# Fused set attention and gated FFN on one core: first batch's stages sorted by the time they can begin, last 24 tiles in six parts of four, idle matmuls in TensorE's wait

One core of one Trainium2 chip. The metric is the device time of one execution in microseconds (us); lower is better. The "span" of a trace is the core's own time from its first to its last instruction, some 1.8 us less.

## The reference

Two attentions in a row (each a batch's tokens against 32 inducing points), then a gated FFN on every token:

```python
def _attn_ref(x, inducing):                  # x: 4 x 12416 x 128, inducing: 32 x 128
    I = np.broadcast_to(inducing[None], (B, m, C))
    def mab(q, kv):
        s = scale * (q @ kv.transpose(0, 2, 1))
        s = s - s.max(-1, keepdims=True)
        a = np.exp(s)
        a /= a.sum(-1, keepdims=True) + 1e-09
        return a @ kv
    h = mab(I, x)                            # "first attention"
    return mab(x, h)                         # "second attention"

def _moe_ref(x, w_gate, w_val, w_out):       # 49664 x 128, d_ff 1536
    gate = np.maximum(x @ w_gate, 0.0)
    val = x @ w_val
    return gate * val @ w_out
```

## The kernel before

The body (the FFN of a batch, and beside it the attention of the next) is one long software pipeline. The change is in what comes ahead of it, the **head**: all of batch 0 has to be loaded (97 tiles of 128 tokens), cast to fp16, transposed, scored against the inducing points, exponentiated and summed, before the first score of the second attention (L178) can begin. A part of the load passes through these stages:

```python
sizes = [8] * 10 + [4] * 3 + [2] * 2           # tiles in each load; the single tile 96 is put in as part 3
...
def turn(j):                                    # transposes (L268, PE) and their copy out of PSUM (L269, DVE)
    for t in range(t0, t1):
        nc.tensor.transpose(ps[:, t - t0, :], x16[:, t, :], eye16)
    nc.vector.tensor_copy(out=xTs(xT, t0, t1 - t0), in_=ps[:, 0 : t1 - t0, :])

for j in range(n_parts + 3):
    if j < n_parts:                             # casts of part j: half on POOL (L280), half on ACT (L281)
        ...
        nc.gpsimd.tensor_copy(out=dst[:, 0:h, :], in_=x32[:, 0:h, :])
        nc.scalar.copy(out=dst[:, h:, :], in_=x32[:, h:, :])
    ...                                         # scores (L290, PE) and exp (L292, ACT) of part j-2
    ...                                         # sums of part j-3 on PE: z1a (L301), z (L311), hT (L314)
    if j < n_parts - 1:
        turn(j)
    ...
idle(idle_ps, 3, ...)                           # three matmuls whose result nobody reads (L262)
hT = finish_h(hT_ps, z1)                        # reciprocal L145, product L147 (DVE)
s2 = s2_pe(hT, xT, (0, 1, 0, 1))                # L178: the second attention, and with it the body, begins
```

So the order on each engine is fixed: casts of part j, scores of part j-2, sums of part j-3, transposes of part j.

The softmax here doesn't subtract the row's maximum and nothing guards it: scores larger than these inputs give would overflow.

## Time and profile before

| Kernel before | |
|---|---|
| three runs ahead of the prediction | 700.35, 700.41, 700.72 us |
| profiled execution | 700.71 us, span 698.9 us, recorded clock of TensorE 0.997 |
| last x tile cast, by POOL | 20.78 us |
| first score of the second attention (L178) | 26.05 us |

In the lines below, the first number is the start in us from the start of the span, the second the busy time of that row, then engine, line, operation, out<-in, shape and count; in brackets stands how long the engine was idle before and what ended the wait.

```profile
5.47 1.03 PE L268 MATMUL xT_ps<-eye,x 128*128 128x128 f16 x8 [0.89 <-POOL x L280]
...
9.06 0.27 PE L301 MATMUL z1a_ps<-p,ones 128*128 128x256 f16 x1
```

Eight transposes take 1.03 us at 5.47, and 0.62 at 14.65 in the prediction's lines. So the kernel begins at half clock too; a z1a matmul of 256 columns takes 0.37 at half clock and 0.27 at full, which makes these rows a clock that can be read off the timeline. In this execution the clock is up by 9.06. (The packed trace's record of clock changes begins with the rise itself, at 8.79; the views count the time before that as full clock.)

### The profile page before, as it was taken

The numbers are of one execution on the slowest core, as the hardware profiler recorded it, in microseconds if no ns is written. First come the engines' busy times: TensorE is split into PE (matmuls) and PEld (weight loads), VectorE is DVE, ScalarE is ACT, GpSimd is POOL, SyncE is SP. The second block draws the span as 40 slices with busy tenths as digits, with TensorE's granted clock in tenths as the row PEclk, the third lists the DMA queues.
The fourth block names the chain that finished last, engine by engine and source line by source line (L and its number), as shares of the span: only waits on it lengthen the run. The fifth ranks groups of instructions, "written<-read, shape, count | busy, mean of one in ns | idle before, by whom it ended". The sixth has DMA issues, their size and how long they took to land.

```text
span 698.9 us, 13946 instructions
## 1 busy us (share of the span) xinstructions
PE 631.5 (90%) x4552; PEld 181.1 (26%) x4552; DVE 676.8 (97%) x617; ACT 672.7 (96%) x1380; POOL 372.5 (53%) x680
## 2 busy tenths in 40 slices
PE   5999998999999999999999999998999898888897
PEld 4522222222222222222222222222222222222224
DVE  4699999999999999999999999999999999999997
ACT  5699999999999999999999999999999999999996
POOL 3628648655186474665247474773424543534443
PEclk9999999999999999999999999999999999999999
DMA  9647876432565957513287785732223231231233
GB/s 349 218 122 175 175 166 169 119 78 67 136 174 156 198 146 170 129 61 77 61 173 189 197 185 139 142 99 70 68 70 85 58 92 56 80 84 53 76 56 91
DMA packets 142633, 87.57 MB, mean 125 GB/s; under 512 B 117184, under 2 KB 125920, under 8 KB 140256
## 3 DMA queue, kind: packets, MB, share of 16 engines
q1 hardware_dynamic: 142368, 86.60, 48.8%
q8 instruction: 35, 0.57, 0.3%
q14 instruction: 38, 0.31, 0.2%
q10 hardware_dynamic: 192, 0.08, 0.0%
HBM read 27.80 MB, written 25.43 MB: 76 GB/s over the span
## 4 chain that ended last, share of the span: by engine, by line
ACT 40%; PE 25%; issue 19%; DVE 13%; DMA 2%; SPq 0%; ACTq 0%; POOL 0%; DVEq 0%
ACT g L982 30%; DVE gv L994 13%; PE o_ps L674 11%; PE v_ps L885 8%; ACT oT L680 6%; PE g_ps L885 3%; DMA gv<-in_x_dram 2%; ACT p2q L194 2%; ACT p1T L533 2%; PE o_ps L741 1%; ACT hgv L169 1%; PE h_ps L599 0%; PE xT_ps L268 0%; PE idle_ps L262 0%; ACT p L189 0%
## 5 line engine op out<-in xcount | busy, mean ns | idle before, releaser
L994 DVE TENSOR_TENSOR gv<-g,v_ps 128x1024 f16<-128x1024 f16 (+1 forms) x578 | 657.2, 1209 | 3.3 <-ACT g L982 1.0
L982 ACT ACTIVATE g<-g_ps 128x512 f16<-128x512 f32 (+1 forms) x1168 | 603.2, 618 | 6.7 <-PE g_ps L885 2.5
L674 PE MATMUL o_ps<-gv,wo 128*128 128x512 f16 x1128 | 352.4, 384 | 45.9 <-ACT oT L680 45.8
L691 POOL TENSOR_SCALAR osb<-o,z2i 128x128 f32<-128x128 f16 x380 | 165.8, 453 | 228.7 <-DMA o<-oT 217.1
L885 PE MATMUL g_ps<-p,hgv 32*128 32x512 f16 x1152 | 282.4, 379 | 0.8 <-ACT g L982 0.5
L885 PE MATMUL v_ps<-p,hgv 32*128 32x512 f16 x1152 | 223.6, 384 | 5.5 <-DVE gv L994 4.3
L885 PEld LDWEIGHTS <-hgv 32*128 32x128 f16 x2400 | 66.8, 91 | 267.2 <-issue 262.9
L674 PEld LDWEIGHTS <-wo 128*128 128x128 f16 x1176 | 80.8, 97 | 212.4 <-issue 198.6
L430 POOL TENSOR_TENSOR z2i<-zt,minus 128x16 f32<-128x16 f32 (+3 forms) x31 | 73.3, 2367 | 0.5
L680 ACT CAST oT<-o_ps 128x512 f16<-128x512 f32 (+1 forms) x98 | 59.1, 603 | 0.1
L423 POOL TENSOR_TENSOR zt<-zt 128x32 f32<-128x32 f32 (+5 forms) x124 | 35.1, 283 | 9.7
L501 POOL CAST x<-x 128x2048 f16<-128x2048 f32 x18 | 34.1, 1892 | 11.4 <-DMA x<-in_x_dram 10.8
L423 POOL TENSOR_TENSOR zt<-p2T 128x256 f32<-128x256 f16 (+3 forms) x31 | 17.5, 563 | 30.7 <-DMA p2T<-p 15.4
L269 DVE COPY xT<-xT_ps 128x1024 f16<-128x1024 f16 (+2 forms) x15 | 8.7, 585 | 9.6 <-PE xT_ps L268 8.6
L577 POOL TENSOR_TENSOR zq<-p1g 128x256 f32<-128x256 f16 x18 | 12.1, 671 | 8.5 <-DMA p1g<-p1T 8.5
L280 POOL CAST x<-gv 128x512 f16<-128x512 f32 (+2 forms) x14 | 7.6, 548 | 11.8 <-DMA gv<-in_x_dram 11.7
L281 ACT CAST x<-gv 128x512 f16<-128x512 f32 (+2 forms) x14 | 7.6, 545 | 6.3 <-DMA gv<-in_x_dram 6.3
L268 PE MATMUL xT_ps<-eye,x 128*128 128x128 f16 x97 | 10.0, 254 | 3.8 <-POOL x L280 3.1
L194 ACT ACTIVATE p2q<-s_ps 128x512 f16<-128x512 f32 x22 | 13.4, 610 | 0.0
L579 POOL TENSOR_TENSOR zq<-zq 128x256 f32<-128x256 f32 x15 | 10.9, 726 | 1.2
L533 ACT ACTIVATE p1T<-s1T_ps 128x512 f16<-128x512 f32 x18 | 11.0, 611 | 0.0
L178 PE MATMUL s_ps<-xT,hT 128*32 128x512 f16 x108 | 10.8, 389 | 0.2
(94 smaller groups left out, 159.2 us busy)
## 6 DMA issues: line engine op xcount, KB each, us to landing
out_dram<-osb SPq DMA_DIRECT2D x95, 256.0 KB, 2.2
x<-in_x_dram SPq DMA_DIRECT2D x18, 1024.0 KB, 5.8
p<-p2q SPq DMA_DIRECT2D x88, 64.0 KB, 2.0
gv<-in_x_dram SPq DMA_DIRECT2D x10, 512.0 KB, 7.1
o<-oT SPq DMA_TRANSPOSE x98, 2.4
gv<-in_x_dram SPq DMA_DIRECT2D x3, 256.0 KB, 10.6
x<-in_moe_w_out_dram SPq DMA_DIRECT2D x1, 768.0 KB, 8.1
x<-in_moe_w_gate_dram SPq DMA_DIRECT2D x1, 512.0 KB, 5.3
```

Of the source, the lines that this page charges most:

```text
L194: nc.scalar.activation(out=p2q, in_=ps, func=AF.Exp, scale=sm_scale)
L423: nc.gpsimd.tensor_tensor(out=dst, in0=v[:, :, :, 0:m], in1=v[:, :, :, m : 2 * m], op=ALU.add)
L430: nc.gpsimd.tensor_tensor(out=z2i, in0=v[:, :, :, 0], in1=minus1[:, 0 : n * g].rearrange("p (n g) -> p n g", n=n), op=ALU.pow,)
L501: nc.gpsimd.tensor_copy(out=s["x16"][:, t0:t1, :], in_=s["x32", q])
L533: nc.scalar.activation(out=p1T, in_=ps, func=AF.Exp, scale=sm_scale)
L577: add(out=z, in0=s["p1g"][q][:, 0:half, :], in1=s["p1g"][q][:, half:, :], op=ALU.add)
L674: nc.tensor.matmul(c["ps"][:, 0:w], wo[:, i, :], gv(i), start=(i == 0), stop=(i == NFF - 1))
L680: nc.scalar.copy(out=oT[:, 0:w], in_=c["ps"][:, 0:w])
L691: nc.gpsimd.tensor_scalar(out=osb[:, t, :], in0=o16[:, t, :], scalar1=zz, scalar2=zz, op0=ALU.mult, op1=ALU.mult,)
L885: nc.tensor.matmul(ps[:, cols], hgv[:, s * P : (s + 1) * P], p2, start=True, stop=True)
L982: nc.scalar.activation(out=g16[:, k * w : (k + 1) * w], in_=ps[:, 0:w], func=AF.Relu)
L994: nc.vector.tensor_tensor(out=dst[:, ks, :], in0=g16[:, ks, :], in1=v[:, ks, 0:w], op=ALU.mult)
```

## The change

Its intent: let each stage stand in the queues where its input should be there by an estimated time, rather than at a fixed distance in parts; make the last parts small and equal; and keep TensorE busy in the wait where x arrives late, so that its clock isn't halved.

```diff
-    sizes = [8] * 10 + [4] * 3 + [2] * 2
+    sizes = [8] * 9 + [4] * 6
...
-    n_big = n_parts - 2
+    n_big = sum(t1 - t0 in (8, 1) for t0, t1 in parts)
...
-    for j in range(n_parts + 3):
-        ...                                    # the loop above
+    def cast(j): ...
+    def score(j): ...                          # p1 has 4 buffers, was 3
+    def sums(j): ...
+    def reduce(j): ...
+    late = [j for j in range(n_parts) if parts[j][0] >= 64 and parts[j][1] < NT][0]
+    for j, (t0, t1) in enumerate(parts):
+        n = t1 - t0
+        landed += n
+        at = 0.16 * landed + (1.4 if j >= late else 0)
+        stages.append((at - (0.6 if j == n_parts - 1 else 0), 0, j, cast))
+        at += 0.1 + 0.065 * n
+        if j == late:
+            idles = lambda j: idle(idle_ps, 3, xT[0][:, 0:4, :].rearrange("p t c -> p (t c)"))
+            stages.append((at, 1, j, idles))
+        stages.append((at, 2, j, turn))
+        if j == n_parts - 1:
+            stages.append((at + 0.3, 3, j, reduce))
+        at += 0.05 * n + 0.5 + 0.068 * n + (0.6 if n > 4 else 0.15)
+        stages.append((at, 3, j, score))
+        at += 0.025 * n + 0.6 + 0.026 * n + (0.6 if n > 4 else 0.3)
+        stages.append((at, 4, j, sums))
+    for _, _, j, f in sorted(stages, key=lambda e: e[0:3]):
+        f(j)
...
-                hq = st([P, P], FP32, "hq", 2)
+                hq = st([P, P], FP32, "hq", 1)
```

`at` is a hand-written model of when data are there: 0.16 us a tile, and a pause of 1.4 us ahead of the part that begins at tile 64.

More of the change, by code (lines that the diff above doesn't have):

```diff
@@ L269, in turn @@
         nc.vector.tensor_copy(out=xTs(xT, t0, t1 - t0), in_=ps[:, 0 : t1 - t0, :])
-    for j in range(n_parts + 3):
-        if j < n_parts:
-            t0, t1 = parts[j]
-            x32 = x32s[j]
-            dst = x16[:, t0:t1, :]
-            if t1 == NT:
-                nc.vector.tensor_copy(out=dst, in_=x32)
-            elif j < n_parts - 1:
-                h = (t1 - t0) // 2
-                nc.gpsimd.tensor_copy(out=dst[:, 0:h, :], in_=x32[:, 0:h, :])
-                nc.scalar.copy(out=dst[:, h:, :], in_=x32[:, h:, :])
-            if j == n_parts - 2:
-                t0, t1 = parts[j + 1]
-                nc.gpsimd.tensor_copy(out=x16[:, t0:t1, :], in_=x32s[j + 1])
-        for i in {n_parts: (j - 2, j - 1), n_parts + 1: ()}.get(j, (j - 2,) if 1 < j < n_parts else ()):
-            t0, t1 = parts[i]
-            ps = bank("g", "s1_ps", [P, 8, M])
-            for t in range(t0, t1):
-                nc.tensor.matmul(ps[:, t - t0, :], xTs(xT, t, 1), indT, start=True, stop=True)
-            p1 = p1s[i] = st([P, 8, M], FP16, "p1", 3)
-            nc.scalar.activation(
-                out=p1[:, 0 : t1 - t0, :], in_=ps[:, 0 : t1 - t0, :], func=AF.Exp, scale=sm_scale
-            )
-        if j > 2:
-            t0, t1 = parts[j - 3]
-            p1, n = p1s[j - 3], t1 - t0
-            if j == n_parts + 2:
-                nc.tensor.matmul(z1, ones32[0:1, :], z1s[0:1, :], start=False, stop=False)
-            if j - 3 < n_big:
-                nc.tensor.matmul(
-                    z1a[:, 0 : n * M],
-                    ones16,
-                    p1[:, 0:n, :].rearrange("p t m -> p (t m)"),
-                    start=j == 3,
-                    stop=j - 3 == n_big - 1,
-                )
-            end = j == n_parts + 2
-            for t in range(n if j - 3 >= n_big else 0):
-                first, last = j - 3 == n_big and t == 0, end and t == n - 1
-                nc.tensor.matmul(z1, ones16, p1[:, t, :], start=first, stop=last)
-            for t in range(n):
-                first, last = j == 3 and t == 0, end and t == n - 1
-                nc.tensor.matmul(hT_ps, x16[:, t0 + t, :], p1[:, t, :], start=first, stop=last)
-        if j < n_parts - 1:
-            turn(j)
-        if j == n_parts - 2:
-            turn(j + 1)
-        if j == n_parts:
-            z1s = st([P, M], FP32, "z1s", 1)
-            nc.vector.tensor_reduce(
-                out=z1s, in_=z1a.rearrange("p (t m) -> p m t", m=M), axis=AX.X, op=ALU.add
-            )
@@ new lines, in cast, with score @@
+    def cast(j):
+        t0, t1 = parts[j]
+        x32, dst, n = x32s[j], x16[:, t0:t1, :], t1 - t0
+        if n == 1:
+            nc.vector.tensor_copy(out=dst, in_=x32)
+            return
+        h = n // 2 if n != 4 or j == n_parts - 1 else 2
+        nc.gpsimd.tensor_copy(out=dst[:, 0:h, :], in_=x32[:, 0:h, :])
+        if h < n:
+            nc.scalar.copy(out=dst[:, h:, :], in_=x32[:, h:, :])
+    def score(j):
+        t0, t1 = parts[j]
+        n = t1 - t0
+        ps = bank("g", "s1_ps", [P, 8, M])
+        for t in range(n):
+            nc.tensor.matmul(ps[:, t, :], xTs(xT, t0 + t, 1), indT, start=True, stop=True)
+        p1s[j] = st([P, 8, M], FP16, "p1", 4)
+        nc.scalar.activation(out=p1s[j][:, 0:n, :], in_=ps[:, 0:n, :], func=AF.Exp, scale=sm_scale)
@@ new lines, in sums @@
+    def sums(j):
+        t0, t1 = parts[j]
+        p1, n, end = p1s[j], t1 - t0, j == n_parts - 1
+        if j == n_parts - 2:
+            nc.tensor.matmul(z1, ones32[0:1, :], z1s[0:1, :], start=False, stop=False)
+        if j < n_big:
+            nc.tensor.matmul(
+                z1a[:, 0 : n * M],
+                ones16,
+                p1[:, 0:n, :].rearrange("p t m -> p (t m)"),
+                start=j == 0,
+                stop=j == n_big - 1,
+            )
+        for t in range(n if j >= n_big else 0):
+            first, last = j == n_big and t == 0, end and t == n - 1
+            nc.tensor.matmul(z1, ones16, p1[:, t, :], start=first, stop=last)
+        for t in range(n):
+            first, last = j == 0 and t == 0, end and t == n - 1
+            nc.tensor.matmul(hT_ps, x16[:, t0 + t, :], p1[:, t, :], start=first, stop=last)
@@ new lines, in reduce @@
+    def reduce(j):
+        nc.vector.tensor_reduce(
+            out=z1s, in_=z1a.rearrange("p (t m) -> p m t", m=M), axis=AX.X, op=ALU.add
+        )
+    z1s = st([P, M], FP32, "z1s", 1)
+    stages = []
+    landed = 0
+    late = [j for j in range(n_parts) if parts[j][0] >= 64 and parts[j][1] < NT][0]
+    for j, (t0, t1) in enumerate(parts):
+        n = t1 - t0
+        landed += n
[12 more added lines that the diff above has]
+        stages.append((at, 4, j, sums))
```

## The prediction

> **What bounds the kernel now.** I read the page's chain of work that ended last, then the busy time by window, then the timeline of the first 28 us. The chain shows that the body belongs to other code:
>
> ```profile
> ACT g L982 30%; DVE gv L994 13%; PE o_ps L674 11%; PE v_ps L885 8%; ACT oT L680 6%; PE g_ps L885 3%; DMA gv<-in_x_dram 2%; ACT p2q L194 2%; ACT p1T L533 2%; PE o_ps L741 1%; ACT hgv L169 1%; PE h_ps L599 0%; PE xT_ps L268 0%; PE idle_ps L262 0%; ACT p L189 0%
> ```
>
> The lines of the change (L268 transposes, and the first batch's scores and sums) have less than 1% each. The busy time by window for the stretch after the first batch says why:
>
> ```profile
> 100.00:650.00 550.00, 503.16 (x3429) 132.83 (x3426) 549.12 (x484) 544.94 (x1117) 297.40 (x534) 1.00 0.47 116
> ```
>
> Columns: window, length, then PE, weight load, DVE, ACT, POOL busy, clock, DMA share, GB/s. DVE is busy 549.12 of 550.00 us. That work is not touched, so the change can only start this body earlier. Its worth is what it takes from the head. Next the timeline of the head, each row with start, duration, line, and in brackets the idle time before:
>
> ```profile
> 14.65 0.62 PE L268 MATMUL xT_ps<-eye,x 128*128 128x128 f16 x8 [0.16 <-POOL x L280]
> ...
> 17.48 0.62 PE L268 MATMUL xT_ps<-eye,x 128*128 128x128 f16 x8 [1.70 <-POOL x L280]
> ...
> 20.07 0.59 PE L268 MATMUL xT_ps<-eye,x 128*128 128x128 f16 x4
> ...
> 20.78 0.40 POOL L284 CAST x<-gv 128x256 f16<-128x256 f32 x1
> ...
> 22.73 0.69 PE L268 MATMUL xT_ps<-eye,x 128*128 128x128 f16 x4
> ...
> 24.24 0.42 DVE L321 TENSOR_REDUCE z1s<-z1a_ps 128x32 f32<-128x256 f32 x1 [0.49 <-PE z1a_ps L301]
> ...
> 25.31 0.36 DVE L145 RECIPROCAL rz<-z_ps 128x32 f32<-128x32 f32 x1 [0.64 <-PE hT_ps L314]
> ...
> 26.05 0.40 PE L178 MATMUL s_ps<-xT,hT 128*32 128x512 f16 x4
> ```
>
> The last x tile is cast at 20.78 to 21.18, but its transpose starts only at 22.73 or a little later, and the first score of the second attention (L178), which starts all the rest, at 26.05. From data to start are 26.05 - 20.78 = 5.27 us. Between 18.77 and 22.74 the chain by time runs without a break through PE. Two things make PE late: it idled 1.70 us for data at 15.8 to 17.5, and it then ran slowly:
>
> ```profile
> 15.63:19.04 3.41, 1.54 (x36) 1.33 (x33) 1.07 (x2) 1.88 (x5) 1.50 (x3) 1.00 1.06 381
> 19.04:22.45 3.41, 3.41 (x66) 3.22 (x64) 1.54 (x3) 2.04 (x7) 2.55 (x7) 0.50 1.03 359
> 12.22:15.63 3.41, 3.23 (x80) 3.01 (x76) 2.12 (x4) 2.17 (x5) 1.23 (x2) 1.00 1.02 402
> ```
>
> I cut these windows at the edges where the clock changed. PE was busy 45% (1.54 of 3.41) in the first, and had half the clock in the whole of the next.
>
> **What the Trainium skill says.** "TensorE: Matmul & The Clock Gate", section "What's actually happening": the clock is halved or restored after free-running windows of 3413 ns, by how busy PE was. The trace agrees: half clock lasted from about 19.04 to 22.45. The same page, "Wait — 56ns, not 53.3ns?": start to start never falls below about 25 ns however small the matmul. The trace agrees: at half and at full clock eight 32-column scores put the next instruction 0.20 to 0.21 us on. So the half clock hurts the transposes and the 256-column sums, not the 32-column ones. "PSUM — Partial Sum Buffer", "Engine vs sequencer instructions": ACT, DVE and POOL queues are strict FIFO and matmuls keep program order. The trace is in keeping with it, so the issue order is the schedule. "DMA: Bandwidth & Descriptors", "Specifications", puts the ceiling at 435 GB/s; the trace has 413 GB/s at 8.8 to 12.2 us, so the loads are near it and cannot be hurried.
>
> **The change, part by part.**
>
> (1) Sizes: nine parts of 8 tiles, the single tile, six of 4, against ten of 8, three of 4, two of 2. Still 16 loads and the same bytes; the last data should land near 20.75 as now. The first of the new small parts covers tiles 72 to 75, half of what landed at 18.06; I place it at 17.42 (halfway from 16.78). Estimated landings of the six: 17.42, 18.06, 18.73, 19.41, 20.09, 20.75. Cost of more parts: the last 24 tiles now have six copies of 0.42 us on DVE (2.52) against 0.69 + 3 x 0.42 + 2 x 0.29 = 2.53: nothing. Sums of the six parts no longer use a 128 or 256-column matmul but 24 matmuls of 32 columns, 24 x 0.025 = 0.6 us of PE, spread out.
>
> (2) Idle matmuls: three of 512 columns before the transposes of tiles 64 to 71. By the same form later (25.17, three in 0.81 us) they fill 0.8 of the 1.70 us wait, and the score and sums before them fill 0.6 more, so PE's next window is busy about 2.9 of 3.41 us (an estimate), as the windows that kept the clock were (79 to 95%). What that is worth: 20 transposes at 107 instead of 56 ns (0.43 against about 0.22 for four), 1.0 us, and three 256-column sums at 0.21 instead of 0.11, 0.3 us: 1.3 us of PE's queue.
>
> (3) Order: by it, the scores and sums stand where their input should be there, rather than at fixed distances of two and three parts; transposes of new tiles stand earlier. To price it I walked the queues in the printed instruction order of the changed kernel, with durations of the trace: 4-tile cast 0.40, ACT free again some 0.08 earlier; transposes of four 0.23 on PE, DVE copy starting 0.44 after their start, 0.42 long, next copy 0.05 later; score of four 0.10 on PE, exp 0.30 after its start, 0.28 long (eight tiles 0.38); sums of four 0.20, of eight 0.32 on PE. A through F are the six small parts, "9" the part of tiles 64 to 71.
>
> - 17.45 transposes 9, copy to 18.79. A's copy queues behind it on DVE to 19.26, B's to 19.73.
> - Score A 19.31, exp A to 19.89. The cast of D landed at 19.41 but stands behind exp A on ACT: done 20.21.
> - Score 9 waits for a PSUM bank that copy B frees: 19.78; score B 19.98. exp 9 to 20.51, exp B to 20.70; on ACT the casts of E and F follow, done 21.02 and 21.34. exp C is behind them: 21.54.
> - Transposes D 20.25; sums A; score C 20.68; transposes E 21.06; sums B; score D 21.49.
> - Transposes F need the bank that exp C frees: 21.59; copy F to 22.45, reduction of the big sums to 22.92.
> - PE: sums 9, sums C, score E, sums D from 21.82 to 22.64; score F 22.64, exp F to 23.22.
> - Sums E with the joining fp32 matmul (0.33 by L299 to L311) 22.97 to 23.50; sums F 23.50. The last sum of z is ready some 0.31 later, the reciprocal starts at 23.81.
> - From reciprocal to L178 it is 26.05 - 25.31 = 0.74 us now, and unchanged: 24.55.
>
> The head ends 26.05 - 24.55 = **1.5 us earlier**. The lower limit of such a tail, with nothing in the way after the last cast at 21.18: transposes and copy 0.9, score and exp 0.63, sums 0.5, then 0.74, gives 23.95, a gain of 2.1 us. The walk loses 0.6 of it to ACT's and PE's order.
>
> (4) Buffers: a fourth p1 buffer costs no time; hq falls from two to one. An hq is written once per pair of chunks, 28 slots of some 1.15 us apart, about 32 us, and read by one POOL addition right after: no wait.
>
> Sum: 700.41 - 1.5 = **698.9 us**.
>
> **The rivals.**
>
> *The weights become the bound.* After x come the weight loads, whose end the change does not move. The first halves are cast by 22.72, before 24.55; the last of the gate and value weights by 26.34 (25.30 plus 1.04), needed by the second L159 group at 28.91 now, 27.4 then. 1.1 us are left, so I expect no wait, though the whole gain of the lower limit would leave only 0.5. If it did bind, the gain would stop at about 1: 699.4.
>
> *The clock falls later.* The windows run freely. The tail has gaps for data and banks on PE; if a window still counts too little, the half clock only moves to the stretch with the last sums, L178, L159 and the idle matmuls, which cost about 0.8 us more there (ten 512-column passes at 0.21 extra would be 2.1, of which the idle ones lie partly in waits). Gain 0.7: 699.7. Against it: no window with PE over 79% busy lost the clock.
>
> *The order is worse than the old one in places.* ACT is strictly in order, and the last cast (F) stands before exp C, which waits for nothing; if data land later than I placed them, everything on ACT shifts. A slip of 0.5 us in the landings gives 699.4.
>
> *The order is better than my walk.* If copies and banks come sooner, up to 698.3.
>
> *The body swallows it.* If in the first slots something fixed in time (the output weights' cast at 27.55 to 29.02, the first loads of the next batch) set the pace, nothing would be gained: 700.4. Against it: the output weights are needed only from slot 10, past 40 us, and the DVE rows from 30.41 on are unbroken.
>
> **Range and chances.** 698.9 with 0.8 either way: the lower end is the limit of the tail (2.1) plus a little run noise (the three runs span 0.37), the upper end has the clock or order rivals. 2% would be 14 us, more than half the head: faster and slower by over 2% have 1% each, and slower only if the buffer reduction in (4) stalled the body, for which I see no path.
>
> **What would show each step.** Right: half-clock slices gone between 19 and 22.5 us; L178's place near 24.5 us; the last x cast still at about 20.8 to 21.3; idle matmuls end before the transposes of tiles 64 to 71; DVE in the body as busy as before and the body as long. Step (2) wrong: clock below 0.9 in any window from 17 to 28 us. Step (3) wrong: clock full, but L178 later than 25.2. The weights rival: POOL's L325 as releaser of PE at the second L159. Wrong altogether: L178 earlier by over a microsecond and the span not.

## The result, and the profile after

Ratios here and below are the mean time of one kernel's fast runs over that of the other's of the same rounds, so not quite the ratio of the medians beside them.

| | runs (us) | median |
|---|---|---|
| before | 700.35, 700.41, 700.72, 699.03 | 700.38 |
| after | 699.82, 699.53, 700.17, 700.41 | 700.00 |

Ratio 0.9998 (95%: 0.9981 to 1.0015): the same time. The prediction had 698.9, range 698.1 to 699.7; the measured 700.0 lies outside.

The body was left alone, as predicted. Busy time by window of the kernel after (columns as in the prediction's window lines):

```profile
100.00:650.00 550.00, 503.74 (x3431) 132.84 (x3431) 549.12 (x484) 545.03 (x1117) 297.61 (x539) 1.00 0.46 116
```

DVE is busy 549.12 of 550 us, the same to the last digit. The half clock of the tail is gone. By single microseconds, before:

```profile
20.00:21.00 1.00, 1.00 (x25) 0.94 (x22) 0.62 (x2) 0.61 (x3) 0.86 (x3) 0.50 0.86 332
21.00:22.00 1.00, 1.00 (x23) 0.94 (x22) 0.36 (x2) 0.72 (x3) 0.74 (x2) 0.50 1.01 395
```

and after:

```profile
20.00:21.00 1.00, 0.93 (x20) 0.79 (x21) 0.74 (x3) 0.57 (x3) 0.73 (x2) 1.00 1.01 397
21.00:22.00 1.00, 0.93 (x24) 0.82 (x23) 0.46 (x2) 1.00 (x6) 0.68 (x2) 1.00 1.01 400
```

The eighth column is the clock: 0.50 against 1.00. Yet L178 has come from 26.05 only to 25.10, not to 24.55. The timeline of the head after shows where it was held up:

```profile
8.70 1.14 PE L268 MATMUL xT_ps<-eye,x 128*128 128x128 f16 x9 [0.70 <-DVE x L275]
...
9.91 0.37 PE L297 MATMUL z1a_ps<-p,ones 128*128 128x256 f16 x1
...
11.72 0.37 PE L297 MATMUL z1a_ps<-p,ones 128*128 128x256 f16 x1
...
13.52 0.28 PE L297 MATMUL z1a_ps<-p,ones 128*128 128x256 f16 x1
...
15.25 1.10 POOL L278 CAST x<-gv 128x512 f16<-128x512 f32 x2 [0.66 <-DMA gv<-in_x_dram]
...
17.61 0.38 ACT L289 ACTIVATE p<-s_ps 128x256 f16<-128x256 f32 x1 [0.57 <-PE s_ps L287]
...
17.68 0.81 PE L262 MATMUL z1a_ps<-xT,eye 128*128 128x512 f16 x3
17.89 1.53 ACT L280 CAST x<-gv 128x512 f16<-128x512 f32 x4
...
19.24 0.40 POOL L278 CAST x<-gv 128x256 f16<-128x256 f32 x1 [1.56 <-DMA gv<-in_x_dram]
...
20.59 0.40 POOL L278 CAST x<-gv 128x256 f16<-128x256 f32 x1 [0.26 <-DMA gv<-in_x_dram]
...
24.35 0.36 DVE L145 RECIPROCAL rz<-z_ps 128x32 f32<-128x32 f32 x1 [0.89 <-PE z_ps L306]
...
25.10 0.40 PE L178 MATMUL s_ps<-xT,hT 128*32 128x512 f16 x4
```

Four things differ from what I had walked through.

- **The half clock at the start lasts until about 13.5 us**, not 9. The z1a rows show it (0.37, 0.37, 0.28), and the clock record has the rise at 13.58. In the walk everything ran at full clock.
- At 8.0 PE stands idle for 0.70 us: the transpose of the single tile is now ahead of that of tiles 16 to 23, and waits for a cast on DVE.
- **The late part is another one.** Tiles 64 to 71 land at about 15.2 (POOL casts them at 15.25), without a pause. The pause comes before tiles 84 to 87 (POOL idle 1.56 us until 19.24). The order assumes it ahead of tile 64.
- ACT casts its half of tiles 64 to 71 only at 17.89, 2.6 us after the data, since in its fixed order the cast stands behind exps of earlier parts, which wait for PE (17.61); PE fills the time with the idle matmuls (17.68), for data that have long been there.

What was right: POOL cast its half of the last x part from 20.59 (landing predicted at 20.75), and from reciprocal to L178 it is 25.10 - 24.35 = 0.75 us (predicted 0.74). ACT's half of that part was done only at 22.05, where the walk had 21.34.

**The distance from L178 to the end is fixed.** Span less start of L178 is 698.9 - 26.05 = 672.85 before and 698.0 - 25.10 = 672.90 after, and 672.85 to 672.96 in all 16 usable traces. So L178's place tells the time of an execution, and nothing of the gain was lost in the body.

### The profile page after: what moved, and what is told of

It reads as the page before. It is cut to its first block, busy times and chain, and to the rows that moved or that the text cites. A ratio compares the mean times of both kernels' runs of the same rounds, so it can differ in the third digit from the quotient of the medians.

```text
span 698.0 us, 13986 instructions
## 1 busy us (share of the span) xinstructions
PE 632.2 (91%) x4571; PEld 181.2 (26%) x4571; DVE 676.6 (97%) x617; ACT 672.8 (96%) x1381; POOL 370.9 (53%) x680
## 4 chain that ended last, share of the span: by engine, by line
ACT 39%; PE 21%; issue 18%; DVE 12%; DMA 7%; POOL 2%; SPq 0%; ACTq 0%; POOLq 0%; DVEq 0%
ACT g L998 29%; DVE gv L1010 12%; PE o_ps L690 10%; PE v_ps L901 7%; ACT oT L696 5%; PE g_ps L901 3%; DMA x<-in_x_dram 2%; DMA gv<-in_x_dram 2%; ACT p2q L194 2%; DMA x<-in_moe_w_out_dram 1%; ACT p1T L549 1%; PE o_ps L757 1%; DMA o<-oT 1%; ACT hgv L169 1%; DMA out_dram<-osb 1%
## 5 line engine op out<-in xcount | busy, mean ns | idle before, releaser
L269 DVE COPY xT<-xT_ps 128x1024 f16<-128x1024 f16 (+1 forms) x15 | 8.6, 584 | 9.0 <-PE xT_ps L268 8.4
L278 POOL CAST x<-gv 128x512 f16<-128x512 f32 (+1 forms) x15 | 7.9, 528 | 11.7 <-DMA gv<-in_x_dram 11.6
L289 ACT ACTIVATE p<-s_ps 128x256 f16<-128x256 f32 (+2 forms) x16 | 5.2, 333 | 6.1 <-PE s_ps L287 5.9
L280 ACT CAST x<-gv 128x512 f16<-128x512 f32 (+1 forms) x15 | 7.4, 532 | 3.7 <-DMA gv<-in_x_dram 3.7
```

## The experiments

There were 15 runs in four groups, on two chips: of eleven new kernels, and of the kernels before and after again. The first three groups have their own runs of the kernel before; the fourth uses the nine of the third and one more. All kernels gave the right result. In most executions the time is 1.7 to 2.0 us more than the span, in some up to 3.0; why isn't shown, so the larger comparisons below use spans. "Clock up by" is the first z1a or score row of the timeline that has the full-clock duration.

The theories at this point, in words: the *pause* theory (the order's pause stands ahead of the wrong part, and a right guess gives the predicted 1.5 us); the *two kinds* theory (the kernel before has two kinds of execution, and I had profiled the slow one); the *beginning* theory (the order is held up by its start, the single tile or the clock). The expectations are quoted as they were written ahead of each group; where they letter theories, the letters are those of that group.

### First group: repeat, and parts of the change (before: nine runs, median 699.41)

**The kernel after again (r_after).**

> The changed kernel once more, unaltered, for more runs and a second trace. Theory A (the head is 0.95 us shorter in every execution, the four first runs were only too few against a spread of 1.7 us): L178 near 25.1 us again, and 0.6 to 1.2 us faster than the kernel before in five rounds. Rival B (the gain is in some executions only, because the late load falls elsewhere in others): L178 anywhere between 24.5 and 26, the times as spread as before and no difference over 0.4 us.

Measured: 699.71, 699.65, 700.01, 701.27, and 2523.82 for the profiled execution, which was spoilt and isn't used. Ratio 1.0010 (0.9996 to 1.0024). In this group the kernel before was at 699.4, not 700.4, and the kernel after stayed where it had been.

**Idle matmuls alone, in the old kernel (e_idle).**

```diff
+            if parts[j][0] == 64:
+                idle(idle_ps, 3, xT[0][:, 0:4, :].rearrange("p t c -> p (t c)"))
         if j < n_parts - 1:
             turn(j)
```

> The kernel before with the three idle matmuls alone, ahead of the transposes of tiles 64 to 71, in the old order and sizes. Theory A (of the 0.95 us most was the half clock): no half clock from 19 to 22.5 us, L178 near 25.0 to 25.2, so as much as the whole change. Rival B (the clock costs little since the tail waits for data anyway): L178 at 25.6 to 26.0, though the clock is full.

Measured: 699.15 to 699.36 in five of five (ratio 0.9997, 0.9985 to 1.0010), L178 at 24.66, no half clock in the tail. Timeline of this kernel:

```profile
9.09 0.37 PE L301 MATMUL z1a_ps<-p,ones 128*128 128x256 f16 x1
...
15.85 0.81 PE L262 MATMUL z1a_ps<-xT,eye 128*128 128x512 f16 x3
16.49 0.61 PE L268 MATMUL xT_ps<-eye,x 128*128 128x128 f16 x8
...
24.66 0.40 PE L178 MATMUL s_ps<-xT,hT 128*32 128x512 f16 x4
```

So L178 is 26.05 - 24.66 = 1.4 us earlier than in the trace of before, and earlier than either theory had it. Not all of that need be the matmuls': a second halved trace (r_before, below) has 25.39. Yet the time is hardly better than that of the nine runs of before. Their recorded clocks say why. Two of the nine have 0.997 and 0.998, and 700.14 and 700.39 us; the other seven have 0.999 or 1.0, and a mean of 699.38. **The kernel before has two kinds of execution**, with and without a window of half clock in its tail, and both its time and the profile that I had read were of the halved kind.

**The change without its idle matmuls (e_noidle).**

```diff
-            stages.append((at, 1, j, idles))
```

> The changed kernel without the three idle matmuls. In its trace they ran at 17.68 to 18.49, where PE would have waited for ACT's cast of tiles 64 to 71 at 18.3 in any case. Theory A (the new order alone keeps PE busy enough in every window): clock full, L178 within 0.15 us of 25.1. Rival B (the idle matmuls hold the clock): a stretch of 3.4 us at half clock somewhere from 19 to 26 us, and L178 at 25.6 to 26.2.

Measured: 699.79, 699.48, 700.83, 699.48, 700.44; ratio 1.0008 (0.9995 to 1.0022). The traced one has full clock in the tail and L178 at 24.75, 0.35 earlier than theory A had it. No loss is seen: with the new order PE's queue is full enough without them.

**The pause put where the trace has it (e_late84).**

```diff
-    late = [... if parts[j][0] >= 64 and ...][0]
+    late = [... if parts[j][0] >= 84 and ...][0]
```

> The changed kernel with its assumed pause in the loads moved from tile 64 to tile 84, where the trace shows it (tiles 64 to 83 landed at 15.2 to 17.3 us, 1.4 us before ACT came to them, the next ones at 19.2). Theory A (ACT's in-order casts behind a wrong place of the pause cost the missing gain): casts of tiles 64 to 71 on ACT at 15.3 instead of 17.9, L178 at 23.6 to 24.2, 0.9 to 1.5 us before the changed kernel's. Rival B (the pause follows PE's instruction fetch and moves again with the order): the late part is another one than tiles 84 to 87, and L178 gains under 0.5 us. Rival C (the last data's landing at 20.6 sets the end): L178 within 0.2 us of 25.1.

Measured: 699.64, 700.26, 700.34, 699.82, 699.94; ratio 1.0008 (0.9995 to 1.0020); L178 at 24.96. ACT did cast tiles 64 to 71 early, at 15.66. It gained nothing, because the last casts now stood behind later exps: POOL cast its half of tiles 84 to 87 at 18.92, ACT at 20.26. Timeline of this kernel:

```profile
20.08 0.28 ACT L289 ACTIVATE p<-s_ps 128x128 f16<-128x128 f32 x1 [0.16 <-PE s_ps L287]
20.26 1.00 ACT L280 CAST x<-gv 128x256 f16<-128x256 f32 x3
```

The pause theory falls.

### Second group: the beginning (before: nine runs, median 699.48)

**The kernel before, traced again (r_before).**

> The kernel before, unaltered, for more executions and a second trace. Theory A (it has two kinds of execution: half clock from about 19 to 22.5 us in some, at spans of 698.4 to 698.9, and full clock in the rest, at 697.4 to 697.7, as the recorded clocks of the nine shared runs suggest): both kinds again, and where the trace has the full clock, L178 at 24.4 to 24.8 us. Rival B (the kernel before always has the half clock, and the fast runs come from something else): a trace with half clock and a span under 697.8.

Measured: 700.08 for the profiled execution (recorded clock 0.998), then 699.22, 699.34, 699.35, 699.39. The trace fell on the halved kind again. Busy time by window:

```profile
19.00:20.00 1.00, 0.95 (x24) 0.74 (x21) 0.96 (x2) 0.68 (x2) 0.71 (x3) 0.84 1.08 404
20.00:21.00 1.00, 1.00 (x20) 0.91 (x18) 0.13 (x2) 0.68 (x2) 0.66 (x3) 0.50 1.07 422
21.00:22.00 1.00, 1.00 (x23) 1.00 (x22) 0.47 (x2) 0.46 (x2) 0.93 (x2) 0.50 1.03 399
22.00:23.00 1.00, 1.00 (x20) 0.84 (x17) 0.82 (x3) 0.34 (x2) 0.30 (x1) 0.50 1.04 313
```

L178 at 25.39. The two kinds theory holds: one kernel, one chip, 700.08 with the half clock in the trace and 699.3 with recorded clocks of 0.999 and 1.0. (The traced span, 698.3, is 0.1 under the range put.) No execution of this kernel with the full clock in its tail was traced: that its L178 is then near 24.7 is inferred from spans (697.59, the mean given under e_warm_b, less 672.9).

**The single tile moved back (e_tile3).**

```diff
-        at = 0.16 * landed + (1.4 if j >= late else 0)
+        at = 0.16 * landed + (1.4 if j >= late else 0) + (1.3 if n == 1 else 0)
```

> The changed kernel with the stages of the single tile 1.3 us later in the order, so that its transpose no longer stands ahead of that of tiles 16 to 23 (PE waited 0.70 us for it at 8.0 us). Theory A (that wait makes PE late from the start, so its instruction fetch and with it the late load come at 16.8 instead of 14.7 us, where the order expects them): the fetch back at 14.6 to 15.2 us, tiles 64 to 71 the late ones again, L178 at 23.9 to 24.5, and 0.4 to 1.0 us faster than the changed kernel. Rival B (PE is late because of the half clock up to 9 to 11 us, the wait itself is caught up): the fetch at 16 us or later and L178 within 0.3 us of 24.8 to 25.1.

Measured: 698.62 (traced), 699.82, 699.79, 700.02, 700.48; ratio 1.0002 (0.9989 to 1.0014). The traced execution has the clock up by 8.6 and L178 at 23.92, which is 1.2 us better than the kernel after; but by their spans (696.8, 698.0, 696.8, 698.0, 698.4) only two of the five are of that kind. Moving the tile isn't what decides alone.

**A warm start (e_warm).** Six 512-column matmuls on a tile of ones, in PE's first wait. `z1a_ps`, which holds their unread result, is allocated earlier for it.

```diff
+    def warm(n):
+        for _ in range(n):
+            nc.tensor.matmul(idle_ps.rearrange("p (k c) -> p k c", c=P), eye16,
+                ones16.unsqueeze(1).broadcast_to([P, BLK // P, P]), start=True, stop=True)
+    warm(4)
     nc.tensor.transpose(indT_ps, ind16, eye16[:M, :M])
+    warm(2)
```

> The changed kernel with six idle matmuls of 512 columns while PE waits for the first data (2.4 to 5.3 us), so that the clock is full earlier. Transposes ran at 1.03 us for eight up to 8.8 to 10.7 us, against 0.61 later. Theory A (the early half clock makes PE late): transposes at 0.6 us for eight from about 7 us at the latest, L178 at 24.0 to 24.5, and a spread below 0.6 us. Rival B (PE waits for data early on, the clock there costs nothing): L178 at 24.7 to 25.1 and the spread as before.

Measured: 698.60, 698.61, 698.50, 698.47, 698.85; ratio 0.9986 (0.9973 to 0.9998). Timeline of this kernel:

```profile
2.43 1.87 PE L119 MATMUL z1a_ps<-ones,eye 128*128 128x512 f16 x4 [2.43 <-DVE ones L107]
...
6.54 0.62 PE L281 MATMUL xT_ps<-eye,x 128*128 128x128 f16 x8 [0.50 <-POOL x L291]
...
8.87 0.27 PE L310 MATMUL z1a_ps<-p,ones 128*128 128x256 f16 x1
...
16.33 0.38 ACT L302 ACTIVATE p<-s_ps 128x256 f16<-128x256 f32 x1 [0.58 <-PE s_ps L300]
...
16.61 1.22 ACT L293 CAST x<-gv 128x512 f16<-128x512 f32 x3
...
23.82 0.40 PE L193 MATMUL s_ps<-xT,hT 128*32 128x512 f16 x4
```

(Its lines are shifted; L193 is L178, L293 is L280.) The eight transposes at 6.54 are already at full clock, and the first score of the second attention begins at 23.82. That is 25.10 - 23.82 = 1.3 us ahead of the kernel after and beyond the limit of 23.95 that I had worked out. (The limit counted from a last cast done at 21.18; in this trace ACT's last one is done at 20.77.)

**Both (e_warm_tile3).** The edits of e_warm and e_tile3 together.

> Both of them. Theory A (both make PE late, in sum): L178 at 23.6 to 24.2 us, near my limit of 23.95, span at 696.5 to 697.1, 0.5 to 1.0 us faster than the kernel before with full clock. Rival B (the last tiles' path through ACT and PE is the limit whatever comes early): L178 not before 24.5.

Measured: 699.00, 698.47, 698.68, 698.56, 698.53; ratio 0.9986 (0.9974 to 0.9999); L178 at 24.14. Nothing beyond the warm start: once the clock is up, the single tile's place doesn't matter.

### Third group: which part of the change earns what, with a warm start (before: nine runs, median 699.28)

**The old order, idle and warm matmuls (e_idle_warm).** The edits of e_idle and e_warm on the kernel before.

> The kernel before (old sizes, old order) with both sets of idle matmuls, those at the start and those in the wait for tiles 64 to 71: the clock alone, full in all executions. Theory A (with a full clock the new sizes and order are worth some 0.7 us): span 697.3 to 697.6 in every execution, L178's counterpart near 24.5 us, so 0.6 to 0.9 us behind the changed kernel with the warm start (696.6 to 697.0). Rival B (the warm start did all of it): span 696.6 to 697.0 here too.

Measured: 699.38, 699.34, 699.89, 699.70, 699.17; ratio 1.0000 (0.9987 to 1.0012); L178 at 24.70, as in e_idle (24.66), though by the clock records the rise came at 7.8 instead of 11.8. The old order has no use for the early clock. (The spans, 697.4 to 698.1, are spread wider than put.)

**The same with the new sizes (e_sizes_idle_warm).**

```diff
-    sizes = [8] * 10 + [4] * 3 + [2] * 2
+    sizes = [8] * 9 + [4] * 6
```

> The same with the new sizes (nine of 8, six of 4), the order still the old fixed distances. Theory A (the order earns, the sizes do not): within 0.25 us of the run with old sizes. Rival B (the sizes earn, through smaller last steps): span under 697.1.

Measured: 698.80, 699.21, 699.27, 698.73, 699.04; ratio 0.9993 (0.9980 to 1.0005); L178 at 24.12. Of the 0.72 us between the means of e_idle_warm (699.50) and of the warm start's ten runs (698.78, with e_warm_b below) the sizes bring 0.49, more than theory A allows. The other 0.23 is what the new order and the rest of the change have left, and so few runs don't resolve it.

**Warm, without the change's idle matmuls (e_warm_noidle).** The edits of e_warm and e_noidle.

> The changed kernel with the warm start but without its own three idle matmuls. Theory A (the new order keeps PE busy by itself, the idle matmuls of the change earn nothing): within 0.2 us of the one with them (median 698.6), no half clock. Rival B (with PE no longer late, its wait for tiles 64 to 75 is real, and without the idle matmuls some executions get the half clock): one or more of five executions 0.5 us or more slower, with a recorded clock of 0.998 or less.

Measured: 698.54, 699.56, 699.14, 698.72, 699.01; ratio 0.9992 (0.9980 to 1.0005); L178 at 23.87; no recorded clock under 0.999. The median is 0.4 us above the 698.6 put down, but the mean span is the warm start's (696.96 against 696.94). Again no sign that the new order needs them.

**Warm, with the pause put at tile 72 (e_warm_late72).** In e_warm the late part was tiles 72 to 75.

> The changed kernel with the warm start and the assumed pause at tile 72, where its trace shows it (tiles 64 to 71 landed at 15.07 us and ACT cast them at 16.61, tiles 72 to 75 landed at 16.69). Theory A (what is left is ACT's cast behind a place of the pause that is one part too early): that cast at 15.1 to 15.3, the first score of the second attention at 23.3 to 23.6 instead of 23.82, span 696.2 to 696.5. Rival B (the fetch, and the pause with it, moves again): no gain over 0.15 us. This is also my attempt at a version that beats both kernels.

Measured: 698.64 (traced), 698.65, 700.19, 700.16, 700.15; ratio 1.0004 (0.9990 to 1.0017); L178 at 23.95 against 23.82. Even where the guess fits the trace, nothing is gained. The three slower executions have recorded clocks of 0.999 and 1.0, and no trace; they stay unexplained. A recorded clock doesn't cover the half clock at the start, so a late rise isn't excluded.

### Fourth group: what stayed open (before: ten runs, median 699.38)

**The kernel after, traced once more (r_after2).**

> The changed kernel, unaltered, with a second usable trace. Theory A (its time hangs on when the clock window lets the clock up in the first 11 us): spans from 697.0 to 698.5 over the executions; in the traced one transposes of eight at 1.0 us up to some time, and the later that time the later L178: 24.3 to 24.8 us if the clock comes up by 8.9 us, 24.9 to 25.6 if later. Rival B (its order is slow whatever the clock does): L178 at 25 us or later with the clock up before 8 us.

Measured: 699.33 (traced), 700.14, 699.63, 700.32, 699.65, 699.49; ratio 1.0005 (0.9992 to 1.0017); L178 at 24.64. The clock was up by 12.9. I had expected 24.9 at least for so late a clock: a miss of 0.26.

**The warm start again (e_warm_b).** The same kernel as e_warm.

> The changed kernel with the warm start once more, on the chip of the others. Theory A: spans 696.5 to 697.1 in all five, 1.0 us or more under the mean of the changed kernel and 0.6 or more under that of the kernel before. Rival B (the first result was luck with the window): two or more executions at 697.6 or more.

Measured: 698.81, 698.52, 698.73, 699.03, 699.68; ratio 0.9992 (0.9979 to 1.0006); L178 at 24.11. With e_warm's five, the mean span is 696.94 (696.6 to 697.8) against 697.95 of the kernel after (14 executions, 697.5 to 698.5) and 697.59 of the full-clock executions of the kernel before (26, 697.2 to 698.0; r_before's with them). **By span the warm start is 1.0 us ahead of the kernel after**, and 0.65 ahead of the kernel before at full clock. This second run alone is less clear: one of its five spans is 697.8, so neither theory's terms are met, and by time it isn't clear of the kernel before. e_warm_tile3 (mean span 696.82) is as fast.

**What makes a part late (e_fetch_warm).** In the view of the DMA queues over one microsecond, one line stands out. Kernel before, 14 to 15 us:

```profile
q8 instruction: 1, 0.02, 6.8%
```

and after, 16 to 17 us:

```profile
q8 instruction: 1, 0.02, 6.9%
```

Columns: packets, MB, share of the 16 engines' time. It is a block of instructions, 6.9% of 16 us, so 1.1 us of one DMA engine's time in these 16 engine-microseconds. "Runtime: NRT & Kernel Launch", section "Instruction fetch mechanics", of the Trainium skill says that an engine's instructions are refilled in blocks of 16 KiB, 256 instructions. In the 16 traces the first packet of the execution starts when PE has begun 146 to 183 pairs of weight load and matmul, and the page of the kernel before counts 35 such packets for 4552 matmuls, so 130 pairs or 260 instructions each: this agrees with PE's stream. To move the packet, I put 48 small matmuls at the start instead of the first four warm ones (1.44 us of PE instead of 1.87; the clock rises at 5.86 instead of 5.63, so hardly later):

```diff
-    warm(4)
+    for _ in range(48):
+        nc.tensor.matmul(idle_ps[:, 0:M], eye16, ones16[:, 0:M], start=True, stop=True)
```

> The changed kernel with 48 idle matmuls of 32 columns at the start in place of four of the six wide ones: nothing else than PE's count of instructions is moved, by 44 pairs. Theory A (the 16 KB instruction packet follows PE's count, and the part in flight is late by it): first packet at 11.3 to 12.6 us, so the late part is one of tiles 48 to 63 and not 72 to 75, and the second packet at 18 to 19.7 us, before the last data, so the last parts are late once more, by 0.6 to 1.3 us, and L178 at 24.6 to 25.3, span 697.5 to 698.3 - the slow kind that e_tile3 and e_warm_late72 had. Rival B (packets come by time, or the lateness has another cause): packets at 14 to 15 and 21 us, tiles 72 to 75 late, span as with the warm start.

Measured: 701.06 (traced, recorded clock 0.997), 699.60, 699.57, 699.54; ratio 1.0006 (0.9992 to 1.0020). The packet came at 12.66 (14.02 in e_warm), and tiles 56 to 63 became the late part. Timeline, then busy time by window of this kernel:

```profile
15.33 0.62 ACT L294 CAST x<-gv 128x512 f16<-128x512 f32 x1 [1.70 <-DMA gv<-in_x_dram]
15.36 0.61 POOL L292 CAST x<-gv 128x512 f16<-128x512 f32 x1 [2.23 <-DMA gv<-in_x_dram]
...
16.03 1.01 PE L282 MATMUL xT_ps<-eye,x 128*128 128x128 f16 x8 [1.61 <-POOL x L292]
```

```profile
17.00:18.00 1.00, 0.85 (x24) 0.69 (x22) 0.69 (x1) 0.38 (x1) 0.67 (x3) 0.50 1.06 389
18.00:19.00 1.00, 1.00 (x19) 0.66 (x17) 0.00 (x0) 0.69 (x2) 0.71 (x2) 0.50 1.10 395
```

So the packet follows PE's instruction count, and the late part follows the packet. PE's wait of 1.61 us then halved the clock, and L178 came at 26.37. One half of my expectation missed: the second packet, at 18.84, did not make the last parts late (19.35, 20.01, 20.67, as regular as before). The three other executions have a span of 697.8, within theory A's range.

### The traces of the new order side by side

| kernel | clock up by | late part begins at tile | ACT casts tiles 64 to 71 | L178 (us) |
|---|---|---|---|---|
| after | 13.5 | 84 | 17.89 | 25.10 |
| e_late84 | 13.0 | 84 | 15.66 | 24.96 |
| e_noidle | 13.0 | 84 | 17.55 | 24.75 |
| r_after2 | 12.9 | 80 | 17.44 | 24.64 |
| e_warm_tile3 | 8.8 | 80 | 16.93 | 24.14 |
| e_warm_b | 9.2 | 64 | 16.89 | 24.11 |
| e_warm_late72 | 7.2 | 72 | 15.08 | 23.95 |
| e_tile3 | 8.6 | 76 | 16.71 | 23.92 |
| e_warm_noidle | 7.2 | 72 | 16.66 | 23.87 |
| e_warm | 7.0 | 72 | 16.61 | 23.82 |

The clock separates the table: all four above 24.6 have it late, all six below 24.2 early. The late part doesn't: at tile 80 there are 24.64 and 24.14, and with an early clock tiles 64, 72, 76 and 80 all give 23.8 to 24.15. By the clock records the rise comes at 13.58, 12.81, 12.48 and 11.90 in the first four rows, in the order of their L178, and at 5.63 to 8.77 in the others. e_tile3's trace has the early clock without any warm matmul, so it isn't the warm matmuls as such. (e_fetch_warm isn't in the table: it also has a half clock in its middle.)

**From ACT's cast of tiles 64 to 71 on, the tail is rigid.** In the eight traces that leave the pause at tile 64 (all but e_late84 and e_warm_late72), L178 starts 7.21 or 7.22 us after this cast, whichever part is late and whenever the last x lands. In the timelines above the cast (17.89, 16.61) stands behind an exp (17.61, 16.33) that waits for PE's scores: so a PE that is late from the start delays ACT, and ACT delays all the rest.

Why the clock came up late in the kernel after can be read too. Busy time by window; the edges are my estimate, 3.41 us and twice that before the clock was up (by the clock record 6.75 to 10.16, with 79%):

```profile
6.69:10.10 3.41, 2.65 (x36) 2.49 (x37) 1.86 (x5) 1.19 (x3) 1.23 (x2) 1.00 1.04 420
```

PE was busy 2.65 of 3.41 us (78%), the clock stayed halved, and the next window (3.21 busy) raised it. In the trace of before, the window 5.40 to 8.81 has 3.02 busy (89%) and raised it at once. The new order's own 0.70 us of waiting for the single tile lies in the window that failed. It isn't the new order alone, though: in e_idle's trace, with the old order, the rise came at 11.76.

## Why the prediction was wrong

**The bound, and that a gain is passed on**: right. Span less L178 is constant to 0.11 us in all traces. The body swallows nothing, and the weights never bound: the second L159 group is released by ACT's `g` (idle 1.29 us, 27.96) after as before.

**The base of the subtraction** failed first. I took 1.5 us, read from an execution of 700.71, off a median of 700.41. By the trace itself, L178 at 24.55 means a span of 24.55 + 672.9 = 697.45 and a time of about 699.25, not 698.9. That is 0.35 of the miss of 1.1.

**Step (3), the walk**, is the rest. Put at 24.55, L178 came at 25.10 and 24.64 in the two traces; the mean span of the first four runs, 698.1, puts it at 25.2, so 0.65 late. (The last 0.1 is time beyond the span, 1.9 in these runs against 1.8.) The term that was mis-sized is PE's queue: the walk used full-clock durations and an empty queue at 17.45, while the half clock of the start lasted to about 13 us and left PE and, behind it, ACT late. The walk let ACT cast tiles 64 to 71 as they land, at 16.78; they had landed by 15.25, but ACT came to them at 17.89, 1.11 us later than put. The tail from there took 7.21 us, 0.56 less than the walk's 24.55 - 16.78 = 7.77. The difference, 0.55, is the miss of L178 in this trace. With the clock up early the same order gives 23.82 to 24.14: then the walk was even too cautious by 0.4 to 0.7. Of the rivals, "the order is worse than the old one in places" came nearest (699.4), through the shift on ACT that it names, but from a late PE and not from late landings. The landing of the parts was wrong as well (the pause moved from tile 64 to tile 84), but the experiments show this to cost little.

**Step (2), the clock in the tail**, was right as a mechanism (no halved execution in the 15 of the three kernels with the old order and these matmuls, against 7 of 33 of the kernel before in these groups) and wrong as a gain. I priced it at 1.3 us. Measured, the halved kind has a mean span of 698.44 (7 executions) against 697.59, so 0.85 us. And it is a matter of chance: it befell three of the four runs that stood first (by their times; only the profiled one has a recorded clock), and 7 of 33 later. So 0.85 x 7/33 = 0.2 us is what removing it is worth on average.

**Steps (1) and (4)**: the last data did land where put (20.59 against 20.75). But I had priced the smaller parts at nothing, and with a warm start they bring 0.5 us. For hq and p1, no wait is seen: the body has the same DVE time.

**The sum, put together anew**: against the full-clock executions of the kernel before, the kernel after is 697.95 - 697.59 = 0.36 us slower; against the halved ones 0.49 faster. A first comparison with three of four halved made this a draw.

**What stays open**: which DMA engine serves the instruction packet, and why the second packet does no harm; the three executions of e_warm_late72 that are 1.5 us slower at full recorded clock; and why the other three runs of e_fetch_warm, at full recorded clock too, are 0.9 us slower than e_warm. That the old order has no use for an early clock is measured; why is not: that its fixed distances between stages set its pace is only argued.

## What to carry to other kernels

Before crediting a gain to the removal of a slow stretch, find out in how many executions the stretch is there: a few runs' recorded clocks would have told it ahead of this prediction. An order tuned to a time line of arrivals is only as good as the state in which the kernel starts, so look at the first windows' matmul durations and, where PE waits for the first data anyway, warm its clock there. Look also for the step from which all the rest follows at a constant distance, as here ACT's cast of tiles 64 to 71: what delays it delays the end. And a pause that a trace shows ahead of one tile may belong to PE's instruction count, and moves when matmuls are added or dropped.

## What the Trainium skill lacked or had wrong

- "TensorE: Matmul & The Clock Gate", section "What's actually happening", lets the clock fall "after ≥1 idle window (~3.4µs)". Here the windows of 3.41 us before a fall had PE busy for 45% (1.54 us, before), 52% (r_before) and 53% (e_fetch_warm, with a wait of 1.61 us); after one with 64% (e_warm, 5.63 to 9.05) the clock stayed. It also gives no share for the way up: 85% (e_warm_tile3, 1.94 to 5.35) did not raise the clock, 88% (before, 5.38 to 8.79) did. The edges are laid from the changes in each trace's clock record.
- The same page, section "Part 4: PE-mode transpose", says that the full clock "doesn't engage" for transposes, which don't count as busy "the same way". Here eight of this kernel's transposes (`nc.tensor.transpose`) take 1.03 us before and 0.61 to 0.62 after the clock is up, so they do run at the full clock; and of the 3.00 us busy in the window that raised it (before, 5.38 to 8.79) 2.78 are transposes.
- No page says that a view of the clock can lack the half clock at the start: it has 1.00 for 5.40 to 8.81 us of the trace of before, where those transposes take 1.03 us. The trace's clock record begins only with the rise, at 8.79.
- "Runtime: NRT & Kernel Launch", section "Instruction fetch mechanics", calls the cost of a new block of instructions "mostly hidden". Its block size agrees (130 pairs a packet), but the first packet, 1.1 us on one of the DMA engines while x is loading, goes with an x part that is 0.9 to 1.6 us late. The second packet of e_fetch_warm, at 18.84 us, did no harm, so the rule is incomplete here too.
